# Float64 weights converted through the bits of their high word, with ScalarE and GpSimd taking a share

## The chip, the core and the metric

The kernel runs on one core of a Trainium2 chip. The metric is the device time of one execution in microseconds. TensorE multiplies matrices into PSUM; VectorE (DVE), ScalarE (ACT) and GpSimd (POOL) work on tiles of 128 partitions; SyncE (SP) issues the transfers. PE stands for TensorE's matmuls and PEld for its weight loads.

## The reference

An FFT filter is followed by two MLPs. `x` is (2, 3008, 256); the result of one stage feeds the next.

```python
X = np.fft.rfft(x, axis=1)
y = np.fft.irfft(X * (filt_r + 1j * filt_i)[None], n=3008, axis=1).astype(np.float32)
x = y.reshape(6016, 256)
h = x @ w_in                               # w_in 256 x 2048
x = ((h / (1 + np.exp(-h))) @ w_out).astype(np.float32)
g = x @ w_gate                             # w_gate, w_val 256 x 1536
out = (((g / (1 + np.exp(-g))) * (x @ w_val)) @ w_out2).astype(np.float32)
```

The filter and `x` are float32. The five weight matrices are float64, since `setup_inputs` scales float32 numbers by a float64 factor. No engine here computes in float64, so the kernel has to make float32 of them: it gets each weight as two 32-bit words, the low word first.

## The kernel before

The FFT of length 3008 is done as 64 x 47 by matmuls, batch 0 first (`F0`), in plain float32. Batch 1 (`F1`) is worked off in pieces between the units of the first MLP. Every number that goes into a product of an MLP is split into a high and a low part (two fp32r tiles), and a product is three matmuls: high by high, high by low, low by high.

The first MLP has **units** (`units`): one unit is a block of 512 tokens by 128 hidden columns. `m1_in` makes six matmuls into a PSUM tile of `psp` (four tiles), a Silu on ScalarE gives `u` (L534), ScalarE casts its high part (L514) and VectorE subtracts to get the low part (L515). `m1_out`, six matmuls into `acc`, comes `LAG = 4` units later. The first 32 units go through the weights in four quarters `q`, two token blocks on each; a quarter's weights of `w_in` (`i1`) and `w_out` (`o1`) must be converted by then. All later units use what is there.

The **conversion** goes by half-tiles of 128 x 512 weights, 34 in all: 16 of `i1` and `o1`, 12 of the second MLP's `g` and `v`, 6 of its `o2`. For one half-tile:

- `load_w`: a 512 KB transfer into `raw` (low and high words in turn).
- `conv_a`: VectorE masks the mantissa bits of the high word into `m` (L401), takes the top 16 bits' exponent (L406), clamps it (L407), moves it to float32's place (L408) and joins it with the sign in a tile `scale` (L409), whose other halves were set to zero at the start.
- `conv_m` (L415): ScalarE turns the mantissa into a float, 1 plus m times 2^-20.
- `conv_b`: VectorE adds the low word times 2^-52 (L420), and GpSimd multiplies by `scale` (L421).
- `conv_c`: ScalarE casts the high part `w` (L429), GpSimd subtracts to get the low part (L430).

The order on each engine is the order in which the code issues the operations (`manual_schedule`): by hand until the first unit, then by `todo`, a list of steps by unit index. `weights(i, key, q, step)` puts `load_w` at i - 2, `conv_a` at i, `conv_b` at i + 1 and `conv_c` at i + 2, and the second half `step` units later. The steps of a unit are issued ahead of its matmuls. Engines work in order, so an operation that waits holds up what stands behind it. Tiles named `mid` come from one pool of 35 buffers, in which a new load waits until an old tile has been read.

The other steps that matter here: `s2` filters a spectrum (matmul, then L293 and two L295 on VectorE into `y` and `t2t`, an add L299 on GpSimd); `turn` transposes, and ScalarE copies the result to `tin` (L254); `s4` finishes the inverse transform, ScalarE casting `xh` (L359) and VectorE subtracting (L360). `split_x` splits an input of batch 1 for `s1`, with a cast on ScalarE (L203) and a subtraction of 96 x 1024 on GpSimd (L204).

## Time and profile before

| | us |
|---|---|
| median of three runs | 1226.03 (1224.44 to 1226.59) |
| the profiled execution | 1226.94 |
| span of its trace | 1225.2 |

| engine | busy us | share | instructions |
|---|---|---|---|
| PE | 1198.5 | 98% | 7068 |
| DVE | 752.6 | 61% | 1202 |
| ACT | 651.8 | 53% | 1171 |
| POOL | 443.1 | 36% | 354 |

The span is what the trace covers of one execution; the profiled time has 1.7 us more, of what lies around it. Busy time of PE is that of a pipeline, so that a busy PE need not be at its pace; the granted clock (PEclk, 1.00 is 2.4 GHz) has to be read beside it. A timeline row has the start, the duration, the engine, the line and the operation, and, in brackets, the idle time of the engine ahead of it and the instruction that ended it. The same operation can have different durations at different places. In the table of stretches the engines stand in the order PE, PEld, DVE, ACT, POOL; in the rows of groups the mean is in ns.

### The profile page before, as it was taken

The page shows a single profiled execution, that of the slowest core. Times are in us where ns is not written, and L with a number is a line of the kernel's source. Part 1 is how long each engine was busy: PE and PEld are TensorE (multiplying, and loading weights), DVE is VectorE, ACT ScalarE, POOL GpSimd, SP SyncE. Part 2 cuts the span into 40 slices and gives each one's busy share as a digit, 9 for nine tenths or more (in the row PEclk, how much of TensorE's full clock was granted, in tenths as well). Part 3 has the DMA queues.
Part 4 walks back from the last instruction along what each step waited for, and adds up shares of the span by engine and source line. Part 5 has one row for each costly group of instructions (what it writes and reads, how often), then busy time and mean ns, then how long its engine had stood idle before and what let it go on. Part 6 is the DMA issues. An engine that isn't in the chain of part 4 may idle for free.

```text
span 1225.2 us, 18420 instructions
## 1 busy us (share of the span) xinstructions
PE 1198.5 (98%) x7068; PEld 1049.2 (86%) x7068; DVE 752.6 (61%) x1202; ACT 651.8 (53%) x1171; POOL 443.1 (36%) x354
## 2 busy tenths in 40 slices
PE   8999999999999999999999999999999999999998
PEld 6467678888888888888899999999999999999998
DVE  3989967774245444544425666666666766676664
ACT  2665666565466556556545445445444554444443
POOL 2545643240034233224312443443434434434432
PEclk8999999999999999999999999999999999999999
DMA  9872523331112522412476011010010110110100
GB/s 220 239 208 61 125 78 103 103 95 64 49 55 97 167 69 78 172 43 97 159 282 232 1 36 35 1 36 6 30 36 1 35 35 1 36 35 1 32 18 13
DMA packets 52534, 97.55 MB, mean 80 GB/s; under 512 B 3712, under 2 KB 28800, under 8 KB 52448
## 3 DMA queue, kind: packets, MB, share of 16 engines
q1 hardware_dynamic: 52448, 96.39, 25.4%
q8 instruction: 55, 0.90, 0.3%
q14 instruction: 31, 0.25, 0.1%
HBM read 60.46 MB, written 35.91 MB: 79 GB/s over the span
## 4 chain that ended last, share of the span: by engine, by line
PE 82%; DVE 5%; ACT 3%; issue 2%; POOL 2%; DMA 1%; POOLq 0%; DVEq 0%; ACTq 0%
PE h L507 19%; PE acc L546 19%; PE y L602 11%; PE acc L689 9%; PE xv L602 8%; PE xg L602 7%; PE acc L693 5%; PE s L346 2%; PE s L182 2%; DVE xrl L589 1%; PE s L179 1%; ACT xrh L588 1%; DMA x<-in_xp_dram 1%; ACT xu L588 1%; POOL m L421 1%
## 5 line engine op out<-in xcount | busy, mean ns | idle before, releaser
L546 PE MATMUL acc<-h,w 128*128 128x512 f32 (+1 forms) x1152 | 292.6, 389 | 2.7 <-DVE h L515 2.7
L515 DVE TENSOR_TENSOR h<-u,h 128x512 fp32r<-128x512 f32 (+1 forms) x192 | 156.8, 818 | 217.8 <-ACT h L514 216.4
L507 PE MATMUL h<-xh,w 128*128 128x512 f32 (+1 forms) x768 | 271.0, 394 | 2.6 <-ACT w L429 1.4
L546 PEld LDWEIGHTS acc<-h,w 128*128 128x128 f32 x1152 | 217.0, 189 | 47.2 <-DVE h L515 3.1
L689 PE MATMUL acc<-w,h 128*128 128x512 f32 x564 | 204.8, 397 | 0.0
L602 PE MATMUL y<-xrh,w 128*128 128x256 f32 (+1 forms) x864 | 190.0, 283 | 0.0
L534 ACT ACTIVATE u<-h 128x512 f32<-128x512 f32 (+1 forms) x192 | 112.7, 587 | 123.0 <-PE h L507 121.3
L507 PEld LDWEIGHTS h<-xh,w 128*128 128x128 f32 x768 | 144.7, 189 | 34.3 <-ACT w L429 1.8
L675 POOL TENSOR_TENSOR h<-sg,h 128x512 fp32r<-128x512 f32 (+1 forms) x72 | 91.4, 1270 | 227.9 <-ACT h L672 226.6
L693 PE MATMUL acc<-w,h 128*128 128x256 f32 x564 | 158.3, 281 | 0.1
L602 PEld LDWEIGHTS y<-xrh,w 128*128 128x128 f32 x864 | 148.2, 189 | 4.0
L507 PE MATMUL h<-xl,w 128*128 128x512 f32 (+1 forms) x384 | 149.7, 390 | 0.0
L649 POOL TENSOR_TENSOR c<-u,s 128x512 f32<-128x512 f32 (+1 forms) x72 | 91.6, 1272 | 130.2 <-DVE u L648 128.0
L689 PEld LDWEIGHTS acc<-w,h 128*128 128x128 f32 x564 | 106.1, 188 | 19.2
L602 PE MATMUL y<-xrl,w 128*128 128x256 f32 (+1 forms) x432 | 121.5, 281 | 0.0
L514 ACT CAST h<-u 128x512 fp32r<-128x512 f32 (+1 forms) x192 | 117.5, 612 | 6.2
L693 PEld LDWEIGHTS acc<-w,h 128*128 128x128 f32 x564 | 106.6, 189 | 0.4 <-POOL h L675 0.4
L602 PE MATMUL xv<-xu,w 128*128 128x256 f32 (+1 forms) x648 | 101.5, 283 | 5.5 <-ACT s L627 5.5
L602 PE MATMUL xg<-xu,w 128*128 128x256 f32 (+1 forms) x648 | 100.1, 281 | 0.0
L602 PEld LDWEIGHTS xv<-xu,w 128*128 128x128 f32 x648 | 87.2, 190 | 7.6 <-ACT s L627 7.5
L658 ACT CAST h<-sg 128x512 fp32r<-128x512 f32 (+1 forms) x72 | 44.1, 613 | 92.0 <-DVE sg L650 92.0
L645 ACT ACTIVATE sg<-xg 128x512 f32<-128x512 f32 (+1 forms) x72 | 42.5, 590 | 94.5 <-DVE xg L642 94.5
(109 smaller groups left out, 1918.4 us busy)
## 6 DMA issues: line engine op xcount, KB each, us to landing
raw<-in_w_out_dram SPq DMA_DIRECT2D x14, 512.0 KB, 6.0
zt<-d SPq DMA_DIRECT2D x16, 384.0 KB, 5.1
x<-in_xp_dram SPq DMA_DIRECT2D x15, 384.0 KB, 9.9
d<-z SPq DMA_DIRECT2D x11, 512.0 KB, 3.3
d<-x SPq DMA_DIRECT2D x22, 256.0 KB, 2.2
x<-d SPq DMA_DIRECT2D x11, 512.0 KB, 4.5
out_dram<-ob SPq DMA_DIRECT2D x11, 512.0 KB, 3.2
w<-dw_g SPq DMA_DIRECT2D x9, 512.0 KB, 6.0
```

The source lines that it names most:

```text
L507: nc.tensor.matmul(ps[:, :n], wt[key, f // 4, g][:, wpart, o:o + P], x[xpart][:, g, :n], start=(g == 0 and k == 0), stop=(g == 1 and k == 2),)
L514: nc.scalar.copy(h[:, 0, :n], u[:, :n])
L515: nc.vector.tensor_tensor(h[:, 1, :n], u[:, :n], h[:, 0, :n], op=ALU.subtract)
L534: nc.scalar.activation(u[:, :n], ps[:, :n], AF.Silu)
L546: nc.tensor.matmul(acc[1, t][m][:, :n], w[:, wpart, o:o + 128], h[:, xpart, :n], start=(f == 0 and k == 0), stop=(f == 15 and k == 2),)
L602: nc.tensor.matmul(o, w_op(key, q, j, n, wpart), x, start=(first and k == 0), stop=(last and k == 2), skip_group_check=True,)
L645: nc.scalar.activation(half(g1), half(xs[0]), AF.Silu)
L649: nc.gpsimd.tensor_tensor(c[:, :, 1, :n], u3, s[:, :, 1, :n], op=ALU.add)
L658: nc.scalar.copy(pack(h[:, 0]), half(g1))
L675: nc.gpsimd.tensor_tensor(pack(hs[1][:, 1]), half(g2), pack(hs[1][:, 0]), op=ALU.subtract)
L689: nc.tensor.matmul(a.rearrange("p (l d) -> p l d", l=2), h[:, 0, i * P:(i + 1) * P], w[:, :, f % 2, :], start=(f_at == 0), stop=False, ski ...
L693: nc.tensor.matmul(a[:, D:], h[:, 1, i * P:(i + 1) * P], w[:, 0, f % 2, :], start=False, stop=(f_at == 11), skip_group_check=True,)
```

## The change

The high word of a float64, read as a float32, has a number's sign and the upper exponent and mantissa bits. The new conversion takes its absolute value as a float and clamps it to the range that float32 can hold, cuts off the top exponent bits, shifts the rest left by three, puts sign and top exponent bit back, and adds the low word's upper three bits as an integer.

- `conv_0` is new, on ScalarE: Abs of the high word into `m` (L400 of the new file), and the low word times 2^-29, written as an integer, into `e` (L401).
- `conv_a`, on VectorE: clamp (L406), mask and shift (L407), sign and top bit (L410). Three operations of 512 four-byte words stand for the five before.
- `conv_b` is GpSimd's alone: an add of 32-bit integers (L416) where there was a float multiply. VectorE's L420 of before is gone.
- `conv_c` is as it was, and so are all matmuls and their order.
- `weights` loads at i - 3 and puts `conv_0` at i - 1. SyncE's list has the same 223 rows; in it one load of `raw` moves ahead of one load of `x`, because of the earlier place.
- The `scale` tiles and their three memsets go. `m` has five buffers for four, `e` three.
- In the part by hand, `conv_a` of `i1`'s second half moves behind `s2(6)`, and `conv_0` steps are set ahead of each `conv_a`.

ScalarE's list grows from 1166 to 1200 rows and VectorE's shrinks from 1089 to 961.


VectorE, batch 0's `s2(5)` and what follows, before (`s_410` is `s2(5)`, `s_446` is `s2(6)`):

```order
L293 TENSOR_TENSOR y<-s_410,fr 128x512
L295 TENSOR_TENSOR t2t_112<-s_410,fi 64x512 x2
L401 TENSOR_SCALAR m<-raw 128x512
L406 TENSOR_SCALAR e<-raw 128x512
L407 TENSOR_SCALAR e<-e 128x512
L408 TENSOR_SCALAR e<-e 128x512
L409 SCALAR_TENSOR_TENSOR scale_114<-raw,e 128x512
L293 TENSOR_TENSOR y<-s_446,fr 128x512
L295 TENSOR_TENSOR t2t_111<-s_446,fi 64x512 x2
```

After (`s_402` is `s2(5)`, `s_435` `s2(6)`, `s_464` `s2(7)`):

```order
L292 TENSOR_TENSOR y<-s_402,fr 128x512
L294 TENSOR_TENSOR t2t_112<-s_402,fi 64x512 x2
L292 TENSOR_TENSOR y<-s_435,fr 128x512
L294 TENSOR_TENSOR t2t_111<-s_435,fi 64x512 x2
L406 TENSOR_SCALAR m<-m 128x512
L407 TENSOR_SCALAR m<-m 128x512
L410 SCALAR_TENSOR_TENSOR m<-raw,m 128x512
L292 TENSOR_TENSOR y<-s_464,fr 128x512
L294 TENSOR_TENSOR t2t_112<-s_464,fi 64x512 x2
```

The conversion stands behind `s2(6)` and not ahead of it, and has three operations and not five.

ScalarE at the same place, before: the cast of the first converted half, then the copies of `turn(6)` and `turn(7)`.

```order
L319 COPY z<-s_406 128x512
L266 ACTIVATE fr<-fr 64x512
L429 CAST w<-m 128x512
L254 COPY tin<-turn 128x512 x2
L319 COPY z<-s_442 128x512
```

After:

```order
L318 COPY z<-s_398 128x512
L265 ACTIVATE fr<-fr 64x512
L424 CAST w<-m 128x512
L400 ACTIVATE m<-raw 128x512
L401 ACTIVATE e<-raw 128x512
L253 COPY tin<-turn 128x512 x2
L318 COPY z<-s_431 128x512
```

The two operations of `conv_0` for the second half came in between the cast and the copies to `tin`.

VectorE where the units begin, before: the last subtraction of `s4`, the rest of one conversion, a second one, and the low parts `h` of units 0 and 1.

```order
L360 TENSOR_TENSOR xl<-s_698,xh 128x104
L420 SCALAR_TENSOR_TENSOR m<-raw,m 128x512
L401 TENSOR_SCALAR m<-raw 128x512
L406 TENSOR_SCALAR e<-raw 128x512
L407 TENSOR_SCALAR e<-e 128x512
L408 TENSOR_SCALAR e<-e 128x512
L409 SCALAR_TENSOR_TENSOR scale_114<-raw,e 128x512
L515 TENSOR_TENSOR h<-u,h 128x512 x2
```

After:

```order
L359 TENSOR_TENSOR xl<-s_685,xh 128x104
L406 TENSOR_SCALAR m<-m 128x512
L407 TENSOR_SCALAR m<-m 128x512
L410 SCALAR_TENSOR_TENSOR m<-raw,m 128x512
L510 TENSOR_TENSOR h<-u,h 128x512 x2
```

The rest of the first conversion (L420) is gone, and the second has three operations ahead of unit 0's `h`.

The diff, without its blank lines:

```diff
 F32 = mybir.dt.float32
 F32R = mybir.dt.float32r
 U32 = mybir.dt.uint32
-U16 = mybir.dt.uint16
 AF = mybir.ActivationFunctionType
 ALU = mybir.AluOpType
...
     wt, late = {}, {}
     SRC = {"i1": w_in, "o1": w_out, "g": w_gate, "v": w_val, "o2": w_out2}
-    scale_t = [stp.tile([P, 512, 2], U16, name=f"scale{i}", bufs=1) for i in range(3)]
-    n_half = [0]
+    TINY, HUGE = (float(np.array(h, np.uint32).view(np.float32)) for h in (0x38000000, 0x47EFFFFF))
     raws, parts, pair = {}, {}, {}
     def load_w(key, q, half):
...
                 src[P * half:P * half + P, 1024 * q:1024 * (q + 1)],
             )
-    def conv_a(key, q, half, on_act=True):
+    def conv_0(key, q, half):
         raw = raws[key, q, half]
-        high, top = raw[:, :, 1], raw.bitcast(U16)[:, :, 3]
-        sc = scale_t[n_half[0] % len(scale_t)]
-        n_half[0] += 1
         if key in ("g", "v"):
             if half == 0:
                 pair[key, q] = mid([P, 2, 512], "v2", U32)
             m = pair[key, q][:, half]
         else:
-            m = stp.tile([P, 512], U32, tag="m", name="m", bufs=4)
-        nc.vector.tensor_scalar(m, high, 0xFFFFF, None, op0=ALU.bitwise_and)
-        parts[key, q, half] = m.bitcast(F32), sc
-        if on_act:
-            conv_m(key, q, half)
-        e = stp.tile([P, 512], U16, tag="e", name="e", bufs=1)
-        nc.vector.tensor_scalar(e, top, 0x7FF0, None, op0=ALU.bitwise_and)
-        nc.vector.tensor_scalar(e, e, 896.0 * 16, 1151.0 * 16, op0=ALU.max, op1=ALU.min)
-        nc.vector.tensor_scalar(e, e, 896.0 * 16, 8.0, op0=ALU.subtract, op1=ALU.mult)
+            m = stp.tile([P, 512], U32, tag="m", name="m", bufs=5)
+        e = stp.tile([P, 512], U32, tag="e", name="e", bufs=3)
+        parts[key, q, half] = m.bitcast(F32), e
+        nc.scalar.activation(m.bitcast(F32), raw[:, :, 1].bitcast(F32), AF.Abs)
+        nc.scalar.activation(e, raw[:, :, 0], AF.Copy, scale=2.0 ** -29)
+    def conv_a(key, q, half):
+        v = parts[key, q, half][0]
+        m, high = v.bitcast(U32), raws.pop((key, q, half))[:, :, 1]
+        nc.vector.tensor_scalar(v, v, TINY, HUGE, op0=ALU.max, op1=ALU.min)
+        nc.vector.tensor_scalar(
+            m, m, 0x07FFFFFF, 3, op0=ALU.bitwise_and, op1=ALU.logical_shift_left
+        )
         nc.vector.scalar_tensor_tensor(
-            sc[:, :, 1], top, 0x8000, e, op0=ALU.bitwise_and, op1=ALU.bitwise_or
+            m, high, 0xC0000000, m, op0=ALU.bitwise_and, op1=ALU.bitwise_or
         )
-    def conv_m(key, q, half):
-        v, _ = parts[key, q, half]
-        nc.scalar.activation(v, v.bitcast(U32), AF.Copy, bias=1.0, scale=2.0 ** -20)
     def conv_b(key, q, half):
-        low = raws.pop((key, q, half))[:, :, 0]
-        v, sc = parts[key, q, half]
-        nc.vector.scalar_tensor_tensor(v, low, 2.0 ** -52, v, op0=ALU.mult, op1=ALU.add)
-        nc.gpsimd.tensor_tensor(v, v, sc.rearrange("p f w -> p (f w)").bitcast(F32), op=ALU.mult)
+        v, e = parts[key, q, half]
+        nc.gpsimd.tensor_tensor(v.bitcast(U32), v.bitcast(U32), e, op=ALU.add)
     def conv_c(key, q, half):
         v, _ = parts.pop((key, q, half))
...
     def weights(i, key, q, step=1):
         for half in range(2):
-            at(max(i - 2, 0), load_w, key, q, half)
+            at(max(i - 3, 0), load_w, key, q, half)
+            at(max(i - 1, 0), conv_0, key, q, half)
             for k, fn in enumerate((conv_a, conv_b, conv_c)):
                 at(max(i + k, 0), fn, key, q, half)
             i += step
-    for i, fn, half in ((1, conv_m, 0), (2, conv_b, 0), (3, conv_a, 1), (4, conv_c, 0), (4, conv_b, 1), (6, conv_c, 1)):
+    for i, fn, half in ((1, conv_0, 1), (2, conv_b, 0), (3, conv_a, 1), (4, conv_c, 0), (4, conv_b, 1), (6, conv_c, 1)):
         at(i, fn, "i1", 1, half)
     for q in range(1, 4):
         weights(8 * q - 2, "o1", q, 2)
...
         nc.sync.dma_start(cst[:, 0:96], consts[:, 0:96])
         F0.load_x(0, 4, 4)
         nc.vector.memset(idle, 0.0)
-        first = stp.tile([P, 512], U32, tag="m", name="m", bufs=4).bitcast(F32)
+        first = stp.tile([P, 512], U32, tag="m", name="m", bufs=5).bitcast(F32)
         nc.vector.memset(first[:, :1], 0.0)
         nc.scalar.activation(first[:, :1], first[:, :1], AF.Silu)
         warm(WARM)
-        for sc in scale_t:
-            nc.gpsimd.memset(sc, 0)
         for i in range(1, 4):
             F0.load_x(i)
         nc.sync.dma_start(cst[:, 96:], consts[:, 96:])
...
         s2(0)
         s2(1)
         s1(4, (1,))
+        conv((conv_0, "i1", 0))
         s2(2)
         conv((conv_a, "i1", 0))
         s1(5)
...
         s1(7)
         s3(2)
         s2(5)
-        conv((conv_c, "i1", 0))
+        conv((conv_c, "i1", 0), (conv_0, "i1", 1))
         F0.prep_g(4)
-        conv_a("i1", 0, 1, False)
         turn(6)
         turn(7)
         s3(3)
         s2(6)
+        conv((conv_a, "i1", 1))
         F0.prep_g(5)
         turn(8)
         turn(9)
...
         s2(7)
         turn(10)
         turn(11)
-        conv((conv_m, "i1", 1))
         s3(5)
         s2(8)
         s3(6)
...
         s3(10)
         F1.s1(0, bank_a, (4,))
         F1.store_s1(0)
+        conv((conv_0, "o1", 0))
         for c in range(3):
             s4(c, (0,), bank_a)
         s3(11)
...
         for f in range(4):
             m1_in_first(0, f)
         F1.s1(1, bank_a, (0,))
-        conv((conv_c, "i1", 1))
+        conv((conv_0, "o1", 1), (conv_c, "i1", 1))
         F1.s1(1, bank_a, (4,))
         F1.store_s1(1)
         conv((conv_a, "o1", 1), (conv_b, "o1", 0))
...
         for c in range(3, 6):
             s4(c, (1,), bank_a)
         conv((conv_b, "o1", 1))
-        conv_a("i1", 1, 0, False)
+        conv_0("i1", 1, 0)
+        conv_a("i1", 1, 0)
         at(1, conv_c, "o1", 0, 1)
         for i in range(len(units)):
```


## Rows read from the trace of the kernel before

**Rows 1.** Stretches: length, busy us (count) by engine, granted PE clock, DMA share, GB/s.

```profile
46.27:53.30 7.03, 4.70 (x8) 1.67 (x8) 6.54 (x10) 2.59 (x5) 3.66 (x4) 0.76 0.58 235
...
77.58:84.64 7.06, 4.35 (x14) 3.15 (x12) 6.88 (x11) 3.39 (x7) 2.83 (x2) 0.76 1.03 354
84.64:113.60 28.96, 28.96 (x127) 23.65 (x126) 28.11 (x39) 17.81 (x32) 13.53 (x10) 1.00 0.31 85
113.60:162.74 49.14, 42.83 (x165) 31.09 (x164) 44.46 (x49) 29.06 (x50) 31.92 (x18) 0.93 0.38 97
162.74:300.00 137.26, 137.26 (x625) 112.65 (x624) 89.73 (x100) 85.87 (x145) 41.91 (x25) 1.00 0.26 83
300.00:600.00 300.00, 300.00 (x1377) 247.79 (x1376) 134.37 (x228) 170.69 (x297) 92.01 (x76) 1.00 0.31 100
```

**Rows 2.** Timeline of PE: start, duration, line, operation, idle time before.

```profile
45.41 1.02 PE L179 MATMUL s<-y,cst 128*128 128x512 f32 x2
48.76 1.47 PE L179 MATMUL s<-tin,cst 128*128 128x512 f32 x2 [2.33 <-DVE t2t L295]
...
53.30 1.02 PE L179 MATMUL s<-y,cst 128*128 128x512 f32 x2
54.15 1.02 PE L179 MATMUL s<-tin,cst 128*128 128x512 f32 x2
...
77.58 0.39 PE L546 MATMUL acc<-h,w 128*128 128x512 f32 x1
80.69 2.50 PE L546 MATMUL acc<-h,w 128*128 128x512 f32 x5 [2.71 <-DVE h L515]
82.99 0.63 PE L507 MATMUL h<-xh,w 128*128 128x512 f32 x1
```

**Rows 3.** Timeline of DVE: `conv_a` in gap one, alone, and before unit 0's `h`.

```profile
41.65 0.43 DVE L401 TENSOR_SCALAR m<-raw 128x512 uint32<-128x512 uint32 x1
...
46.61 0.69 DVE L293 TENSOR_TENSOR y<-s,fr 128x512 f32<-128x512 f32 x1
...
65.34 0.42 DVE L401 TENSOR_SCALAR m<-raw 128x512 uint32<-128x512 uint32 x1
...
67.42 0.41 DVE L401 TENSOR_SCALAR m<-raw 128x512 uint32<-128x512 uint32 x1
...
79.96 1.27 DVE L515 TENSOR_TENSOR h<-u,h 128x512 fp32r<-128x512 f32 x2
```

**Rows 4.** Timeline of DVE: one conversion and two units in the full stretch.

```profile
101.85 1.53 DVE L401 TENSOR_SCALAR m<-raw 128x512 uint32<-128x512 uint32 x1
...
104.08 1.27 DVE L408 TENSOR_SCALAR e<-e 128x512 uint16<-128x512 uint16 x1
...
106.69 0.68 DVE L420 SCALAR_TENSOR_TENSOR m<-raw,m 128x512 f32<-128x512 uint32 x1
107.29 0.68 DVE L515 TENSOR_TENSOR h<-u,h 128x512 fp32r<-128x512 f32 x1
107.89 1.51 DVE L401 TENSOR_SCALAR m<-raw 128x512 uint32<-128x512 uint32 x1
```

**Rows 5.** Timeline of POOL: the same multiply undisturbed and in the full stretch.

```profile
62.05 1.27 POOL L421 TENSOR_TENSOR m<-m,scale 128x512 f32<-128x512 f32 x1 [5.01 <-DVE m L420]
...
101.42 1.68 POOL L421 TENSOR_TENSOR m<-m,scale 128x512 f32<-128x512 f32 x1 [2.26 <-DVE m L420]
```

**Rows 6.** Groups of POOL, 113.60 to 162.74: count, busy us, mean ns, idle before.

```profile
L204 POOL TENSOR_TENSOR fl<-x,fh 96x1024 fp32r<-96x1024 f32 x5 | 12.5, 2503 | 1.3 <-ACT fh L203 1.1
```

**Rows 7.** Timeline of ACT around 40 us, and a conversion's scaling copy.

```profile
39.82 0.62 ACT L429 CAST w<-m 128x512 fp32r<-128x512 f32 x1
40.34 1.07 ACT L254 COPY tin<-turn 128x512 f32<-128x512 f32 x2
...
65.80 0.63 ACT L415 ACTIVATE m<-m 128x512 f32<-128x512 uint32 x1 [0.67 <-DVE m L401]
```

**Rows 8.** Instructions on tile `raw`: its loads' time to landing.

```profile
DMA to landing us min/median/max: 3.5/5.5/12.0
```


## The prediction

> **What bounds the kernel now.** I read four views, in this order: the table by stretches, the timeline of TensorE in the stretches that are not full, the timeline of the engine that it waits for there, and the grouped lines of that stretch. In the table the reader should look at TensorE's busy time against the length of the stretch, and at PEclk beside it. From 84.64 to 113.60 and from 162.74 to 600 TensorE is busy all the time at PEclk 1.00 [rows 1]. The first of these has 127 matmuls in 28.96 us, 0.228 us each: that is the full pace of a 512-column product. One unit of the first MLP has 12 of them (six in, six out), 2.74 us, and two units take 5.47 us. Three stretches before 162.74 are not full, and all three show VectorE busy for over nine tenths.
>
> *Gap one, 46.27 to 53.30.* Each pair of spectrum products takes 0.85 us at full pace (53.30 to 54.15). After the pair at 45.41, three pairs should end at 48.8, but the next full-pace pair starts at 53.30 [rows 2]: 4.5 us are lost, partly as idling (2.33 us on VectorE's t2t), partly at PEclk 0.76 [rows 1], that is, some of it at the lower of the two clock levels, 1.2 GHz, after the idling. VectorE was inside the five conversion operations of i1 half 1, 41.65 to 46.61, 4.96 us, while a result waited [rows 3].
>
> *Gap two, 77.58 to 84.64.* The first output product waits 2.71 us for `h` L515, and the six matmuls end at 82.99 and not 1.37 us after 77.58: 4.0 us lost [rows 2]. L515 stands behind another conversion on VectorE and starts at 79.96 [rows 3].
>
> *Gap three, 113.60 to 162.74.* 165 matmuls at 0.228 us are 37.6 us; 49.14 us passed, so some 11 us are lost, again partly at the lower level (PEclk 0.93) [rows 1]. VectorE is busy 44.46 of 49.14.
>
> **Why VectorE is late there.** Two units and one conversion take it from 101.85 to 107.89, 6.04 us against TensorE's 5.47 [rows 4]; it falls behind all through the full stretch, and the bill comes at 113.60. Alone, the five operations of `conv_a` take 2.08 us (65.34 to 67.42) [rows 3]; here L401 takes 1.53 and L408 1.27 [rows 4]. They end just after the GpSimd operation that started at 101.42 and ended at 103.10 [rows 5], which itself took 1.68, not the 1.27 of the row at 62.05: these two engines exclude each other for much of their work. So I add them up. Per half-tile VectorE has 2.08 for `conv_a`, 0.60 for L420 (106.69 to 107.29) and twice 0.60 for L515 (107.29 to 107.89) [rows 4], in all 3.88; GpSimd has twice 1.27 [rows 5], 2.54. The sum 6.42 against 6.04 seen: about 94% of the sum is what the pair needs.
>
> **The change part by part.** *VectorE* loses five narrow operations and L420 and gets three: two tensor-scalar on 512 words, priced by L401's 0.41 alone [rows 3], and one with two tensors, 0.60 as L420 [rows 4]: 1.42 to 1.5 for 2.68, 1.2 us less per half, before any waiting. Its pair sum becomes (1.44 + 1.20 + 2.54) x 0.94 = 4.87 for two units, now below 5.47. With the transforms of batch 1, one every 2.5 units, TensorE has 36 matmuls (8.2 us), and GpSimd one more subtraction of 2.50 us [rows 6]: before (1.25 x 6.42 + 2.50) x 0.94 = 9.9, after (1.25 x 5.18 + 2.50) x 0.94 = 8.4. So five transforms cost 8.5 us too much before and 1 after.
>
> *GpSimd* does an integer add where it did a float multiply. No row has an integer operation there. The nearest is that multiply, 1.27 [rows 5], same shape, two inputs, four-byte words: I take 1.27. The ends are 0.60, what VectorE has for two tensors (L420), and twice the multiply, 2.54; at that end the sum per transform is (1.25 x 6.45 + 2.50) x 0.94 = 9.9, and gap three stays as it is. The three memsets that go ran at the start, when nothing waited for GpSimd: 0.
>
> *ScalarE* gets Abs and a scaling copy for one scaling copy: one operation more per half, priced by L415 (0.63) [rows 7], twice that if reading every other word is slow; below zero is excluded, since an operation is added. In gap three it was busy 29.06 of 49.14 [rows 1]; 6 or 7 halves add 4 us, so it has room. But it works in order, and in three places the pair now stands ahead of something urgent. One is behind the cast at 39.82, ahead of the two `tin` copies at 40.34 [rows 7]: TensorE's next spectrum product comes 1.1 us later (2.5 at the upper price). Another is ahead of the first casts of `s4`, the third ahead of unit 0's Silu; behind that one wait `h`, L510 and the first output product. ACT's list shows one table load, as before, so Abs costs no second one.
>
> *What a rule says of this.* ScalarE takes 0.63 for 512 words, and VectorE 0.41 [rows 3, 7]. The Trainium skill, ScalarE: Activation LUTs, section Rules for kernel authors, says to put such plain arithmetic on VectorE, which it has at up to about three times the rate; the rows show 1.5 times for four-byte words. By that rule the two operations would go to VectorE, the pair sum per transform would be (1.25 x 6.08 + 2.50) x 0.94 = 9.5 against 8.2, and some 5 us of the gain would be gone. The rows speak for ScalarE here, because it is not the engine that is short.
>
> *DMA.* The weight loads are issued one unit earlier and the first reader comes one unit earlier, so two units, 5.5 us, stay between them; landing took 3.5 to 12.0, median 5.5 [rows 8]. ScalarE now waits instead of VectorE. Behind it stand that unit's Silu and cast; TensorE notices only when the four PSUM tiles of `psp` are full, about three units later. On SyncE's list one weight load moves ahead of one `x` load; I put both at 0, and up to 2 us of gap three if the cover fails.
>
> *Where the gains land.* Gap one: VectorE's string from 41.65 loses 4.96 + 0.7 and gets 1.5, up to 2.8 with one wait for GpSimd, and starts 1.0 later because of `tin`; that is 1.9 to 3.1 less, I take 2.6 (ends: -1.3, if the ScalarE delays eat it all, and 4.5). Gap two: L510 stands behind three operations, not five, and VectorE comes there earlier; but ScalarE's pair delays the Silu by 1.2. I take 1.2 left of 4.0: 2.8 (ends 0 and 4.0). Gap three: 1 from the transforms and 1 for ScalarE's order left of 11: 9 (ends 4 and 11). The 18 halves of the second MLP lie in 300 to 600, where TensorE is full and VectorE at 134 of 300 [rows 1]: 0. Past 600 nothing changes.
>
> Sum: 2.6 + 2.8 + 9.0 = 14.4. The profiled execution took 1226.94 us, the median of the runs is 0.9 below it: 1226.94 - 14.4 - 0.9 = 1211.6, so **1212**.
>
> **The rivals.** *ScalarE takes VectorE's place:* the three delays (1.1, 1.2, 1.2) all show in full, and in gap three the cast of `w` waits for GpSimd in front of the next Silu as it does now, so 6 us of 11 stay lost. Gain some 8: 1218. For it: in-order, 60% busy with waits. Against: those waits were for work that VectorE had queued too late. *All gaps close:* 4.5 + 4.0 + 11 = 19.5, 1206.5; against it speaks the `tin` delay. *The gaps belong to the transforms of batch 1* and not to the conversions, and the first two only move: within a microsecond or two, 1225; the period of 6.04 against 5.47 speaks against it. *Slower:* the integer add is dear on GpSimd. It stands in the pair sum in full: at 2.6 us it eats what VectorE saves (1.24 + 1.27); at three times the multiply, 3.8 us, the sum per transform is (1.25 x 7.71 + 2.50) x 0.94 = 11.4, 1.5 over before, 7.6 us for five; and in the stretch from 84.64, 7.25 against 5.47 leaves some 6 more than the lag now. With 5 kept in the first two gaps that gives about 1234. Nothing in the rows shows an integer add, so it can't be excluded.
>
> **How the numbers follow.** Forecast (1208 to 1215) 0.58; all gaps close (below 1208) 0.14; ScalarE's place (1215 to 1221) 0.15; no change 0.06; slower 0.07. About 0.2%, 2.5 us, is what a measurement of this kernel tells from no change: faster 0.87, same 0.06, slower 0.07. An integer add at its upper end would leave the first two gaps' 5.4: 1220.6. The range 1205 to 1221 takes that in, with the forecast and most of its two neighbours, some 0.83.
>
> **What would show it.** Right: PEclk 1.00 and TensorE full from about 75 to 600; the conversion on VectorE in three operations, 1.5 to 2.8 us together; no wait of TensorE for `w`. Wrong: the integer add above 2 us; Abs or the copy above 1 us; TensorE waiting for `u`, `tin` or `xh` of ScalarE, or for a raw weight's load; the gap at 113.60 still there with VectorE idle.

## The result, and the profile after

The changed kernel takes 1211.45 us, median of four runs (1209.42 to 1211.58), beside 1226.31 for the kernel before on the same chip: ratio 0.9878, interval [0.9861, 0.9895]. 1212 was predicted. Run again, the same program gave 1210.40 (ratio 0.9873 [0.9860, 0.9886]). The total is right; none of its three terms is: two were put too small, and the third, up to unit 0, came out with the wrong sign. That is what the experiments are about.

The table by stretches of the changed kernel (columns as in [rows 1]):

```profile
core 0: us, PE busy (x) PEld busy (x) DVE busy (x) ACT busy (x) POOL busy (x), PEclk, DMA share, GB/s
46.00:54.00 8.00, 5.81 (x16) 2.25 (x14) 7.77 (x11) 3.91 (x7) 4.11 (x4) 1.00 0.66 256
75.40:79.05 3.65, 3.20 (x15) 2.24 (x13) 2.06 (x4) 3.59 (x8) 0.53 (x1) 1.00 0.99 253
79.05:111.80 32.75, 32.08 (x140) 25.88 (x139) 30.36 (x32) 27.83 (x49) 21.48 (x14) 1.00 0.43 141
111.80:160.00 48.20, 48.20 (x222) 38.77 (x221) 37.44 (x35) 35.72 (x63) 32.27 (x18) 1.00 0.46 118
```

Set against [rows 1]: PEclk is 1.00 in all of them, and from 111.80 to 160.00, where the kernel before lost some 11 us, TensorE is busy 48.20 of 48.20. In 46 to 54 it still stands for over 2 us, and VectorE is as full as before (7.77 of 8.00).

TensorE's own timeline of the changed kernel (start, duration, line, operation, matmuls; in brackets the idle time ahead and who ended it), its stops of more than 0.2 us up to unit 4, with some rows beside them:

```profile
41.62 1.13 PE L178 MATMUL s<-tin,cst 128*128 128x512 f32 x2 [0.97 <-ACT tin L253]
51.70 1.13 PE L178 MATMUL s<-y,cst 128*128 128x512 f32 x2 [2.04 <-POOL y L298]
69.25 1.55 PE L345 MATMUL s<-cst,zt 96*128 96x94 f32 x12 [0.61 <-DMA zt<-d]
76.20 0.50 PE L502 MATMUL h<-xh,w 128*128 128x512 f32 x1 [0.45 <-ACT u L529]
77.69 1.52 PE L541 MATMUL acc<-h,w 128*128 128x512 f32 x6
80.49 1.53 PE L541 MATMUL acc<-h,w 128*128 128x512 f32 x6
89.29 0.50 PE L502 MATMUL h<-xh,w 128*128 128x512 f32 x1 [0.67 <-POOL w L425]
```

The stop of 2.33 us of [rows 2] has become 0.97 and 2.04; the stop of 2.71 ahead of the first `acc` is gone; a wait for `w` now stands at 89.29, where the kernel before had its waits for `w` at 115.83 (1.38 us) and 117.27 (0.70).

To compare kernels I use four marks on this timeline: the first block of `turn` matmuls after 34 us (T), the first `acc` product of unit 0, of unit 1 and of unit 24. The lengths between them, from the profiled execution of each kernel (before: 39.22, 77.58, 84.64, 169.42; after: 38.75, 77.69, 80.49, 153.92), are called gap one, two and three from here on. Those of the prediction lie inside them: 46.27 to 53.30, 77.58 to 84.64 and 113.60 to 162.74.

| kernel | T at | T to unit 0 (gap one) | unit 0 to 1 (gap two) | unit 1 to 24 (gap three) | unit 24 to end |
|---|---|---|---|---|---|
| before | 39.22 | 38.36 | 7.06 | 84.78 | 1055.8 |
| changed | 38.75 | 38.94 | 2.80 | 73.43 | 1055.6 |
| e12, changed again | 37.67 | 38.93 | 2.78 | 73.24 | 1055.8 |
| e1, no multiply | 40.57 | 38.07 | 4.39 | 74.33 | 1055.5 |
| e2, extra add | 38.86 | 38.90 | 3.50 | 81.38 | 1055.9 |
| e3, on VectorE | 37.48 | 39.85 | 4.35 | 79.26 | 1055.8 |
| e4, old places | 35.72 | 38.23 | 2.74 | 76.27 | 1056.1 |
| e6, i1 later and casts earlier | 41.40 | 34.93 | 2.72 | 74.96 | 1055.6 |
| e7, third operation | 39.29 | 42.39 | 3.45 | 74.15 | 1055.7 |
| e8, late loads | 39.12 | 39.71 | 2.78 | 73.24 | 1055.7 |
| e9, i1 later | 38.67 | 36.69 | 2.77 | 73.32 | 1055.9 |
| e10, i1 and first u later | 38.66 | 42.07 | 3.90 | 73.32 | 1055.9 |
| e11, before, i1 later | 37.79 | 37.73 | 7.66 | 84.54 | 1055.9 |

The change gave 11.35 us in gap three and 4.26 in gap two, lost 0.58 in gap one, and the rest of the 15.7 us between the spans (1225.2 and 1209.5) is T, 0.47, and the end, 0.2. e5 is missing: its profiled execution had a granted clock of 0.75 from end to end, and the same program was run again as e9. Gaps two and three repeat within 0.2 us in the changed kernel, e8 (which edits loads alone), e9 and e12; gap three in e10 too. Gap one does not always repeat: e12 has the changed kernel's length, but e8, whose order up to unit 0 is the same, has 39.71, with PEclk 0.88 in 46 to 54 where the changed kernel had 1.00. T does not repeat either, of which more at the end.

### The profile page after: what moved, and what is told of

It reads as the page before. It is cut to its first block, busy times and chain, and to the rows that moved or that the text cites. A ratio compares the mean times of both kernels' runs of the same rounds, so it can differ in the third digit from the quotient of the medians.

```text
span 1209.5 us, 18403 instructions
## 1 busy us (share of the span) xinstructions
PE 1189.7 (98%) x7068; PEld 1046.4 (87%) x7068; DVE 709.4 (59%) x1100; ACT 668.1 (55%) x1205; POOL 441.5 (37%) x351
## 4 chain that ended last, share of the span: by engine, by line
PE 87%; ACT 4%; DVE 4%; issue 3%; DMA 2%; POOL 1%; SPq 0%; POOLq 0%; DVEq 0%; ACTq 0%
PE acc L541 21%; PE h L502 21%; PE y L597 12%; PE acc L684 9%; PE xv L597 8%; PE xg L597 7%; PE acc L688 5%; PE s L181 2%; PE s L345 2%; DMA fi<-in_fi_dram 1%; DVE xrl L584 1%; DMA raw<-in_w_in_dram 1%; ACT xrh L583 1%; ACT xu L583 1%; DVE sg L645 1%
## 5 line engine op out<-in xcount | busy, mean ns | idle before, releaser
L510 DVE TENSOR_TENSOR h<-u,h 128x512 fp32r<-128x512 f32 (+1 forms) x192 | 168.0, 879 | 244.8 <-ACT h L509 244.4
L541 PE MATMUL acc<-h,w 128*128 128x512 f32 (+1 forms) x1152 | 289.6, 387 | 0.0
```

The lines of the kernel that those rows point to most:

```text
L510: nc.vector.tensor_tensor(h[:, 1, :n], u[:, :n], h[:, 0, :n], op=ALU.subtract)
L541: nc.tensor.matmul(acc[1, t][m][:, :n], w[:, wpart, o:o + 128], h[:, xpart, :n], start=(f == 0 and k == 0), stop=(f == 15 and k == 2),)
```

## Experiments: what gap three is made of

**e1: the kernel before without GpSimd's multiply.** VectorE keeps all its instructions.

```
 def conv_b(key, q, half):
     ...
-    nc.gpsimd.tensor_tensor(v, v, sc.rearrange("p f w -> p (f w)").bitcast(F32), op=ALU.mult)
```

> The kernel before, with GpSimd's multiply by the scale left out of every conversion (the weights stay unscaled, so the output is not the reference's). VectorE's instructions are all as before. Theory A (VectorE and GpSimd exclude each other, so what counts is the sum of both): the sum for two units falls from 6.42 to 3.88 + 1.27 = 5.15, times 0.94 is 4.84, below TensorE's 5.47; with a transform (1.25 x 5.15 + 2.50) x 0.94 = 8.4 against 8.2, as for the changed kernel. The loss at 113.60 to 162.74 goes nearly in full, the first two gaps stay: 1213 to 1217 us. Theory B (VectorE's own five operations are what is too long, GpSimd does not matter): VectorE's 3.88 is unchanged, the loss stays, 1225 to 1227 us.

Measured: 1214.25 us, ratio 0.9889 [0.9874, 0.9903]. Gap three falls from 84.78 to 74.33 although VectorE's five operations are untouched: theory A. That the gaps belong to the transforms of batch 1 is out with it, since none of these was touched. Gap two, which was to stay, falls from 7.06 to 4.39: with the same five operations ahead of it, unit 0's `h` keeps TensorE waiting 1.37 us and not 2.71. VectorE and GpSimd of e1, one conversion:

```profile
89.74 0.42 DVE L406 TENSOR_SCALAR e<-raw 128x512 uint16<-128x512 uint16 x1
93.47 0.42 DVE L401 TENSOR_SCALAR m<-raw 128x512 uint32<-128x512 uint32 x1
98.47 0.42 DVE L401 TENSOR_SCALAR m<-raw 128x512 uint32<-128x512 uint32 x1
98.80 1.52 DVE L406 TENSOR_SCALAR e<-raw 128x512 uint16<-128x512 uint16 x1
```
```profile
98.68 1.36 POOL L429 TENSOR_TENSOR w<-m,w 128x512 fp32r<-128x512 f32 x1 [3.64 <-ACT w L428]
```

One conversion and two units take 5.00 us (93.47 to 98.47), where [rows 4] had 6.04 and the sum promised 4.84. The instruction of 0.42 us (89.74) lasts 1.52 where GpSimd's subtraction starts just ahead of it (98.80, 98.68).

**e2: one more integer add on GpSimd in the changed kernel.**

```
 def conv_b(key, q, half):
     v, e = parts[key, q, half]
     nc.gpsimd.tensor_tensor(v.bitcast(U32), v.bitcast(U32), e, op=ALU.add)
+    nc.gpsimd.tensor_tensor(e, e, e, op=ALU.add)
```

> The changed kernel with one more integer add on GpSimd per half-tile, behind the one it has, on the tile e that nobody reads afterwards (the output stays as it is). Its duration should be that of the add, 1.27 us alone. Theory A (sum of VectorE and GpSimd): 5.18 + 1.27 = 6.45 for two units, times 0.94 is 6.06, as the 6.04 seen before the change; the loss in gap three comes back nearly in full, 11 to 12 us, the first two gaps stay as they now are: 1221 to 1225 us. This is also the run for the rival that a dear integer add makes the change worth little (at 2.5 us it was to eat what VectorE saves). Theory B (VectorE alone): GpSimd's own load is only 2 x 1.27 + 1.27 = 3.8 of 5.47, so nothing moves, 1211 to 1213 us.

Measured: 1219.90 us, ratio 0.9938 [0.9922, 0.9955], a little under the range of theory A. An add whose result nobody reads, on an engine with room (3.8 us of 5.5 by its own count), costs 7.95 us in gap three (81.38 against 73.43): theory B is out. But 11 to 12 were expected. VectorE of e2, then GpSimd:

```profile
94.63 1.26 DVE L406 TENSOR_SCALAR m<-m 128x512 f32<-128x512 f32 x1
97.98 2.39 DVE L511 TENSOR_TENSOR h<-u,h 128x512 fp32r<-128x512 f32 x2
100.29 1.26 DVE L406 TENSOR_SCALAR m<-m 128x512 f32<-128x512 f32 x1
```
```profile
98.14 1.68 POOL L416 TENSOR_TENSOR m<-m,e 128x512 uint32<-128x512 uint32 x1 [1.09 <-DVE m L410]
99.89 1.37 POOL L417 TENSOR_TENSOR e<-e 128x512 uint32<-128x512 uint32 x1
101.22 1.48 POOL L426 TENSOR_TENSOR w<-m,w 128x512 fp32r<-128x512 f32 x1
```

The period is 5.66 us (94.63 to 100.29), not 6.06, only 0.13 over TensorE's two units (2.765 each where it is full). So the factor 0.94 that I carried over is not a constant. The sums and the periods are 5.15 and 5.00 in e1 (one GpSimd operation a half), 6.42 and 6.04 before (two), 6.00 and 5.60 in e3 below (two), 6.45 and 5.66 here (three): the part that overlaps is 0.15, 0.38, 0.40 and 0.79 us, that is 0.15 to 0.26 for each GpSimd operation. In these stretches the two engines shut each other out, but for about 0.2 us for each GpSimd operation.

The Trainium skill, SBUF — State Buffer, section Terms, has this as a port pair that the two share by a lock, held for a whole instruction, where the loser is fully blocked. For the operations of these stretches the trace agrees but for those 0.2 us; some others of VectorE are not held up at all (see gap one).

The period shows the sum; the 7.95 us do not show it alone. In GpSimd's order the added add also stands ahead of other work (99.89, ahead of 101.22). Of the 6.06 us that TensorE waits in gap three of e2 (0.67 in the changed kernel), 4.55 end with GpSimd, the longest wait with `fl`, behind which PEclk is 0.91 in 120 to 140:

```profile
128.46 0.71 PE L181 MATMUL s<-fl,csp 96*96 96x512 f32 x1 [1.91 <-POOL fl L203]
```

How much of the loss comes through GpSimd's own queue and how much through VectorE, e2 does not tell. e3 adds nothing to GpSimd's queue, and loses 5.8 us there all the same.

This run also prices the rival of a dear add: with 2.54 us of integer adds per half the change would still gain 0.62%, near the 1220.6 that the prediction gave for that end.

**e3: Abs and the scaling copy on VectorE.**

```
-    nc.scalar.activation(m.bitcast(F32), raw[:, :, 1].bitcast(F32), AF.Abs)
-    nc.scalar.activation(e, raw[:, :, 0], AF.Copy, scale=2.0 ** -29)
+    nc.vector.tensor_scalar(m, raw[:, :, 1], 0x7FFFFFFF, None, op0=ALU.bitwise_and)
+    nc.vector.tensor_scalar(e, raw[:, :, 0], 29, None, op0=ALU.logical_shift_right)
```

> The changed kernel with Abs and the scaling copy on VectorE, as an and with 0x7FFFFFFF and a shift right by 29, 0.41 us each alone, at the same places in the program. This is what the Trainium skill, ScalarE: Activation LUTs, section Rules for kernel authors, would have: plain arithmetic on VectorE. Theory A (sum of VectorE and GpSimd): 5.18 + 0.82 = 6.0 for two units, times 0.94 is 5.64 against 5.47, and with a transform (1.25 x 6.0 + 2.50) x 0.94 = 9.4 against 8.2: some 5 to 6 us of gap three come back, 1215 to 1219 us. If ScalarE's pair was what cost the most in the changed kernel (its delay of tin, of the first u), the gain there outweighs it: 1209 to 1211 us.

Measured: 1220.80 us, ratio 0.9942 [0.9927, 0.9957]: half of the gain is gone. Gap three has 5.8 us of it, as theory A had, though VectorE's own operations are 3.46 us of 5.53 and GpSimd's 2.54; gap two has another 1.55 and gap one 0.9, which theory A had not, so that the median lies above its range. On VectorE of e3 the operation of 0.41 lasts 1.52, beside a GpSimd operation that started at 96.91 and took 1.68:

```profile
94.13 1.51 DVE L406 TENSOR_SCALAR m<-m 128x512 f32<-128x512 f32 x1
97.35 1.52 DVE L400 TENSOR_SCALAR m<-raw 128x512 uint32<-128x512 uint32 x1
99.73 1.54 DVE L406 TENSOR_SCALAR m<-m 128x512 f32<-128x512 f32 x1
```

The period is 5.60 us (94.13 to 99.73), 5.64 by the sum. The Trainium skill, ScalarE: Activation LUTs, section Rules for kernel authors, would have put the two operations there (its factor of three is for bf16); this run doesn't bear that out for a VectorE that is short.

**e4: the new arithmetic at the old places.** The core of the edit:

```
-            at(max(i - 3, 0), load_w, key, q, half)
-            at(max(i - 1, 0), conv_0, key, q, half)
+            at(max(i - 2, 0), load_w, key, q, half)
+            at(max(i, 0), conv_0, key, q, half)
...
-        conv((conv_c, "i1", 0), (conv_0, "i1", 1))
+        conv((conv_c, "i1", 0))
         F0.prep_g(4)
+        conv((conv_0, "i1", 1), (conv_a, "i1", 1))
         turn(6)
```

> The changed kernel's arithmetic at the places of the kernel before: loads two units ahead and not three, ScalarE's pair right ahead of VectorE's three operations, and those of i1 half 1 ahead of turn(6) as before. Theory A (the arithmetic makes the gain): VectorE now stands up to 1.2 us waiting for ScalarE's pair at each half, but it is the sum with GpSimd that counts and 4.87 + 1.2 = 6.1 is only reached where nothing else of VectorE is queued: 1211 to 1215 us. Rival (the gain hangs on taking ScalarE's pair one unit ahead): VectorE's wait comes on top at every half, two units take 6.1 as before the change, gap three comes back: 1219 to 1224 us.

Measured: 1212.71 us, ratio 0.9881 [0.9865, 0.9896]. The arithmetic makes the gain. The places are worth 2.8 us in gap three (76.27 against 73.43), where VectorE now stands for ScalarE's pair (6.8 us in nine waits); the medians can't tell that apart. The 0.7 us less in gap one is no more than that length moves by itself (e8).

**e8: the loads two units ahead, ScalarE's pair where the change has it.**

```
-            at(max(i - 3, 0), load_w, key, q, half)
+            at(max(i - 2, 0), load_w, key, q, half)
```

> The changed kernel with the weight loads issued two units ahead, as before the change, and not three; ScalarE's pair still comes one unit ahead of VectorE. One unit, 2.77 us, is then between the issue of a load and its first reader; landing took 3.5 to 12.0 us before the change. Theory (ScalarE stands waiting 1 to 9 us at such halves, and TensorE's cover of about three units is used up at the longer ones): 1 to 5 us over the changed kernel, in the stretch from unit 0 to unit 24. Rival (the cover is enough; the earlier load was not needed): within 1 us of the changed kernel.

Measured: 1212.26 us, ratio 0.9869 [0.9852, 0.9886]; gap three 73.24. The earlier loads are worth nothing, so the 2.8 us of e4 are the pair's place.

**e7: a third ScalarE operation.**

```
     nc.scalar.activation(m.bitcast(F32), raw[:, :, 1].bitcast(F32), AF.Abs)
+    nc.scalar.activation(m.bitcast(F32), m.bitcast(F32), AF.Abs)
```

> The changed kernel with a third ScalarE operation in every conversion (Abs of m once more, in place, 0.6 to 0.67 us; the output stays). Theory A (ScalarE has room): the two places where TensorE waits for ScalarE (tin, the first u) grow by 0.65 each, from unit 0 on nothing changes by more than 1 us: 1 to 2.5 us over the changed kernel. Rival (ScalarE, in order and with waits for GpSimd in it, is the next bound): ScalarE's two units hold 2 x 1.25 for Silu and cast, 1.3 for the pair, 0.6 for w and its wait; with 0.65 more the stretch from unit 0 to unit 24 loses 4 us or more: 1217 us or more.

Measured: 1217.26 us, ratio 0.9908 [0.9892, 0.9924]. The time is the rival's, 1217 or more, and not theory A's, but the loss is not where the rival put it: gap three takes 0.72 us and gap two 0.65, so ScalarE has room there, and the rival's 4 us are not to be seen. Ahead of unit 0 it costs 3.45 where 1.3 was expected. TensorE's two waits in e7:

```profile
42.82 1.12 PE L178 MATMUL s<-tin,cst 128*128 128x512 f32 x2 [1.62 <-ACT tin L253]
80.19 0.50 PE L503 MATMUL h<-xh,w 128*128 128x512 f32 x1 [1.47 <-ACT u L530]
```

They grow by 0.65 and 1.02. All waits of gap one together grow by 1.96 us, from 4.40 to 6.36. The other 1.49 are time in which TensorE is busy: PEclk is 0.91 in 40 to 60, 1.00 in the changed kernel. It falls behind the same wait of 2.04 us that the changed kernel has, and the three pairs from 52.89 on take 4.37 us, where three at full pace take 2.58. That this fall comes from the added operation is not shown; e8 had it without one.

## Experiments: why gap one gave nothing

VectorE in gap one of the changed kernel, then GpSimd:

```profile
42.79 0.69 DVE L292 TENSOR_TENSOR y<-s,fr 128x512 f32<-128x512 f32 x1 [1.63 <-PE s L178]
44.84 0.41 DVE L406 TENSOR_SCALAR m<-m 128x512 f32<-128x512 f32 x1
45.29 1.39 DVE L407 TENSOR_SCALAR m<-m 128x512 uint32<-128x512 uint32 x1
46.71 1.41 DVE L410 SCALAR_TENSOR_TENSOR m<-raw,m 128x512 uint32<-128x512 uint32 x1
48.14 0.69 DVE L292 TENSOR_TENSOR y<-s,fr 128x512 f32<-128x512 f32 x1
```
```profile
45.07 1.32 POOL L298 TENSOR_TENSOR y<-y,t2t 128x512 f32<-128x512 f32 x1 [0.26 <-DVE t2t L294]
46.35 1.22 POOL L270 TENSOR_TENSOR fi<-fi,cst 128x512 f32<-128x512 f32 x1
```

The three operations take 3.30 us (44.84 to 48.14), 1.5 alone: two GpSimd operations stand in their way, not the one I allowed for. Ahead of them VectorE idles 1.63, 0.97 of it TensorE's wait for `tin`. What it saved over [rows 3], 4.96 - 3.30, is spent by that idle time.

Not all of VectorE's work is shut out, though. In the same gap, VectorE's two lines of `s2` and a GpSimd add:

```profile
50.27 0.69 DVE L292 TENSOR_TENSOR y<-s,fr 128x512 f32<-128x512 f32 x1
50.97 1.39 DVE L294 TENSOR_TENSOR t2t<-s,fi 64x512 f32<-64x512 f32 x2
```
```profile
50.38 1.26 POOL L298 TENSOR_TENSOR y<-y,t2t 128x512 f32<-128x512 f32 x1 [2.80 <-DVE t2t L294]
```

The add runs beside both, and none of the three is slower than alone: the 24 instructions of L292 in the whole program last 0.690 to 0.693 us, the 48 of L294 0.683 to 0.694, beside GpSimd or not. Both lines read `s`, which lies in PSUM; the conversion and the low parts `h`, which stretch, read SBUF alone. That this is the reason was not tried. The sum of the two engines holds for the operations that stretch, and only for them.

**e5 and e9: the conversion of i1 half 1 out of the gap**:

```
-        conv((conv_c, "i1", 0), (conv_0, "i1", 1))
+        conv((conv_c, "i1", 0))
...
-        conv((conv_a, "i1", 1))
         F0.prep_g(5)
...
         turn(11)
+        conv((conv_0, "i1", 1))
...
-        conv((conv_b, "i1", 1))
+        conv((conv_a, "i1", 1), (conv_b, "i1", 1))
```

> The changed kernel with the conversion of i1 half 1 taken out of gap one: ScalarE's pair behind the tin copies of turn(11), VectorE's three operations behind the last y of s2(11). From the third transposition of turn (38.75 us in the changed kernel's profile) to the first output product of unit 0 (77.69) it took 38.94 us, before the change 38.36: gap one gave nothing. Theory C (the conversion sits where VectorE is the bound: it is busy without a break from 43.51 to 59.9, and the tin copies wait 1.0 us behind ScalarE's pair): that stretch becomes 1.0 + 2.0 us shorter, 35.5 to 37 us, and the median falls by 2 to 3 us below the changed kernel's. Rival (what comes next is late anyway: the second half of zt, which TensorE waits for at 69.25, or the first u): 38.5 to 39.5 us, median within 1 us of the changed kernel's. From unit 0 on nothing should move (76.2 us from unit 0 to unit 24).

> The kernel of the earlier run with i1 half 1 later, whose profiled execution had a granted clock of 0.75 from end to end. Seen so far where i1 half 1 is later together with a second move: 34.93 us from the third transposition of turn to unit 0's first output product (38.94 in the changed kernel) and 77.68 from unit 0 to unit 24 (76.23). Theory C: the move of i1 half 1 alone gives 3 to 3.6 of the 4.0 (35.3 to 36 us, the rest being the wait for the first u, 0.45), and leaves the stretch from unit 0 at 76.0 to 76.6: the median falls 2.5 to 4 us below the changed kernel run beside it. Rival (the second move made it): 38 us or more.

e5: ratio 0.9853 [0.9826, 0.9881]. e9, the same program: 1208.99 us (1204.85 to 1213.70), ratio 0.9857 [0.9836, 0.9878]. Gap one falls to 36.69, 2.2 us less, and the three operations behind the last `y` take 1.6 us in all (56.74 to 58.38). That is between theory C, 35.3 to 36, and its rival, 38 or more. Beside the changed kernel on that chip (e12, 1210.40) the median is 1.4 us lower, less than the 2.5 to 4 expected, and the intervals overlap: that the move gains anything is not shown by the times. TensorE of e9, and what is late next:

```profile
57.16 1.58 PE L345 MATMUL s<-cst,zt 96*128 96x94 f32 x12 [0.92 <-DMA zt<-d]
73.86 0.50 PE L502 MATMUL h<-xh,w 128*128 128x512 f32 x1 [0.80 <-ACT u L529]
```

Both waits are new or longer (0.45 for `u` in the changed kernel): the first half of `zt` comes by DMA when it comes.

**e6: the same, the next weight's pair behind the first Silu, and the casts of `w` one unit earlier.**

```
-    for i, fn, half in ((1, conv_0, 1), (2, conv_b, 0), (3, conv_a, 1), (4, conv_c, 0), (4, conv_b, 1), (6, conv_c, 1)):
+    for i, fn, half in ((1, conv_0, 0), (1, conv_a, 0), (2, conv_b, 0), (2, conv_0, 1), (3, conv_a, 1), (3, conv_c, 0), (4, conv_b, 1), (5, conv_c, 1)):
...
-        conv_0("i1", 1, 0)
-        conv_a("i1", 1, 0)
```

> As the run with i1 half 1 later, and in addition the conversion of the next weight (i1, q = 1): ScalarE's pair of half 0 and VectorE's three go behind unit 0's Silu and cast (which waited for them, 0.45 us of TensorE), ScalarE's pair of half 1 one unit later, and both casts of w one unit earlier (TensorE waited 0.67 us at 88.6 for the second). If these waits are what they seem, 0.5 us less up to unit 0 and 0.7 to 0.9 less between unit 0 and unit 24 (75.4 in place of 76.2): together 3 to 4 us below the changed kernel's median. If the casts now stand waiting for GpSimd in front of Silu, it is no better than the run with i1 half 1 later alone, within 0.5 us.

Measured: 1211.50 us, ratio 0.9856 [0.9834, 0.9878]. Gap one is 34.93, the shortest seen (4.0 less), but unit 1 to 24 takes 1.5 more, and T came at 41.40. By the ratios no better than e9, and no 3 to 4 us below the changed kernel.

**e10: e9 with the next weight's half 0 behind the first Silu, the casts left alone.**

```
-    for i, fn, half in ((1, conv_0, 1), (2, conv_b, 0), ...
+    for i, fn, half in ((1, conv_0, 0), (1, conv_a, 0), (1, conv_0, 1), (2, conv_b, 0), ...
...
-        conv_0("i1", 1, 0)
-        conv_a("i1", 1, 0)
```

> As the run with i1 half 1 later, and the conversion of i1, q = 1, half 0 behind unit 0's Silu and cast; the rest of the order as in the changed kernel. Theory: 0.45 us less up to unit 0 (34.9 us), and from unit 0 on 76 to 76.8, since the casts of w stay where they are: 0 to 0.5 us below the run with i1 half 1 later. Rival (the 1.45 us that the stretch from unit 0 lost in the run with both moves comes from this one): 77.5 us there, and 1 us above it.

Measured: 1211.18 us (1204.96 to 1215.83), ratio 0.9872 [0.9846, 0.9899]. Unit 1 to 24 is 73.32, so e6's loss there came from the casts, or from half 1's pair, which e6 moved too. From unit 0 to unit 24, which the expectation speaks of, it is 77.22, above the theory's 76.8 and just under the rival's 77.5: gap two is 3.90, with a wait of 0.88 us for `u` at 83.13. Gap one of the profiled execution, the slowest of the six, is 42.07. TensorE of e10, and its line by stretches:

```profile
58.76 2.88 PE L345 MATMUL s<-cst,zt 96*128 96x94 f32 x12 [2.53 <-DMA zt<-d]
61.42 1.97 PE L178 MATMUL s<-y,cst 128*128 128x512 f32 x2
63.19 2.71 PE L345 MATMUL s<-cst,zt 96*128 96x94 f32 x12
```
```profile
58.00:70.00 12.00, 11.24 (x38) 9.33 (x39) 4.23 (x12) 2.80 (x9) 1.26 (x1) 0.57 0.71 200
```

TensorE waited 2.53 us for `zt`, and then ran at PEclk 0.57, that is mostly at 1.2 GHz, to about 69: the 12 matmuls of 63.19 take 2.71, those of e9 at their place 1.47. Waits with a lower clock behind them were part of gaps one and two of the kernel before, too [rows 1, 2]. Up to some 3 us before unit 0, e10 has e9's order on every engine, and T came at the same time (38.66 and 38.67); but the loads of `zt` were issued at 54.76, in e9 at 53.14. So most of the 5.4 us between the two profiles is chance, and not the edit. A kernel that comes early to a transfer can pay for it twice, and that fits the wide spread of e9's and e10's times.

**e11: the kernel before, with its i1 half 1 moved the same way.**

```
-        conv_a("i1", 0, 1, False)
         turn(6)
...
-        conv((conv_m, "i1", 1))
...
-        conv((conv_b, "i1", 1))
+        conv_a("i1", 0, 1, False)
+        conv((conv_m, "i1", 1), (conv_b, "i1", 1))
```

> The kernel before, its arithmetic unchanged, with the conversion of i1 half 1 moved as in that run: VectorE's five operations and ScalarE's one behind the last y of s2(11), not ahead of turn(6). If gap one is a matter of the place and not of the arithmetic, the stretch from the third transposition to unit 0 falls from 38.36 to 34.5 to 36.5 us here too, and gaps two and three stay (91.8 us from unit 0 to unit 24): median 2 to 4 us below the kernel before. Rival (the old conversion, 2.1 us on VectorE and one wait for ScalarE, now delays xl and with it the first h as much): within 1 us of the kernel before.

Measured: 1225.69 us, ratio 0.9999 [0.9988, 1.0010]: no gain. Gap one is 0.63 shorter, gap two 0.60 longer; `zt` was 1.53 us late, and PEclk fell to 0.93 in 60 to 80. So the rival's time is right, though not its reason: TensorE has no wait for `xl` in gap one. In this execution the place was no lever by itself, since `zt` and `h` set the pace next.

**e12: the changed kernel beside e9 to e11.**

> The changed kernel itself, on the same chip as the three runs beside it, since its first product of unit 0 lay at 38.94 us behind the third transposition while that transposition itself lay anywhere from 35.7 to 41.4 us in the kernels so far, whose programs are alike up to there. Expected: 38.5 to 39.7 us for the first stretch, 76.0 to 76.4 from unit 0 to unit 24, 1055.5 to 1056.2 from there to the end; the ratio to the kernel before again 0.986 to 0.9895. If the stretches moved by more than this from one execution to the next, differences of less than 1 us between kernels could not be read from single profiles.

Measured: 1210.40 us, ratio 0.9873; all stretches as expected. T, for which nothing was expected, lay at 37.67.

## Why the prediction was right, and where it was not

- **What bounds it: right** for the conversion and the units. VectorE and GpSimd as one resource is what e1, e2 and e3 show, each from another side. One of the readings behind it was loose: L401 ends just after the GpSimd operation named there, but L408 (104.08 to 105.35) after another, which started at 103.83 and took 1.37. The period of two units was to be 4.87. In the changed kernel's full stretch it is 4.80, with VectorE now waiting for ScalarE's `h` in it, while GpSimd's add runs:

```profile
97.74 0.41 DVE L406 TENSOR_SCALAR m<-m 128x512 f32<-128x512 f32 x1
99.62 0.69 DVE L410 SCALAR_TENSOR_TENSOR m<-raw,m 128x512 uint32<-128x512 uint32 x1
101.39 1.22 DVE L510 TENSOR_TENSOR h<-u,h 128x512 fp32r<-128x512 f32 x1 [0.48 <-ACT h L509]
102.54 0.41 DVE L406 TENSOR_SCALAR m<-m 128x512 f32<-128x512 f32 x1
```

- **Gap three: too small.** 9.0 predicted, 11.35 measured in unit 1 to 24, with 0.9 us of a new wait for `w` taken off. The 1 us left for ScalarE's order and the 1 for the transforms did not show, and the gap itself was some 12 and not 11.
- **Gap two: too small.** 2.8 predicted, 4.26 measured, all that there was. TensorE waits 0.45 for the first `u` (76.20), not 1.2, and by the marks this wait falls in gap one. The fewer operations ahead of `h` are not the whole cause: e1 keeps all five and gains 2.67 without the multiply.
- **Gap one: wrong, 2.6 predicted, -0.6 measured.** The step that failed is "1.9 to 3.1 less, I take 2.6". Its `tin` delay of 1.1 was right (0.97); the conversion's 1.5, "up to 2.8 with one wait for GpSimd", was 3.30 with two waits; and the 0.7 that it takes off beside the 4.96 was not there to take: by its size it is L420, and in the kernel before this half's L420 ran later:

```profile
61.29 0.68 DVE L420 SCALAR_TENSOR_TENSOR m<-raw,m 128x512 f32<-128x512 uint32 x1
```

With what was measured, the same sum is 4.96 - 3.30 - 0.97 = 0.69, and 0.57 us less is what shows at the first `h` (63.05 against 64.09, that is 24.30 and 24.87 behind T). It went to longer waits for `zt` (0.61, before 0.19) and the first `u` (0.45, before none). Over the whole of gap one TensorE waits 4.40 us, before 2.72, and needs 1.10 us less for its work, with PEclk 1.00 and not 0.96: -0.58 in all. The lower end, -1.3, "if the ScalarE delays eat it all", names the case. The sum that I used for gap three was not used for the conversion here, although GpSimd is busy for half of that stretch (4.11 of 8.00).

- **The prices: right.** The integer add takes 1.26 us alone and 1.67 where it starts beside VectorE, as the multiply ([rows 5]: 1.27 and 1.68). Abs and copy take 0.67 and 0.66, 0.63 predicted. The add alone, then the changed kernel's groups between 84 and 160 us (line, engine, operation, count, busy us, mean ns):

```profile
55.89 1.26 POOL L416 TENSOR_TENSOR m<-m,e 128x512 uint32<-128x512 uint32 x1
```

```profile
L416 POOL TENSOR_TENSOR m<-m,e 128x512 uint32<-128x512 uint32 x11 | 18.5, 1680 | 11.5 <-DVE m L410 11.5
L400 ACT ACTIVATE m<-raw 128x512 f32<-128x512 f32 x10 | 6.7, 666 | 0.0
L401 ACT ACTIVATE e<-raw 128x512 uint32<-128x512 uint32 x10 | 6.6, 659 | 0.0
```

- **Loads at 0, the second MLP at 0: right** (e8; unit 24 to the end is 1055.5 to 1056.1 in all kernels). **No wait for `w`: wrong**, 0.67 us.
- **The sum:** 2.6 + 2.8 + 9.0 = 14.4 against -0.6 + 4.3 + 11.35 = 15.0, and 0.7 from T and the end. The errors, 3.2 too much and 3.8 too little, nearly cancel, and that is luck; the time came out within 1 us because of it.

## What to carry to other kernels

See in the trace which of VectorE's operations get longer beside GpSimd's (here those that read SBUF alone, not those that read PSUM). Add these and GpSimd's work per period, and allow some 0.2 us of overlap for each GpSimd operation; an operation moved to ScalarE leaves this sum, one that is moved to VectorE enters it (e3). Use the sum wherever such operations meet, in a ramp as in a steady stretch. A stretch that gets shorter is worth what the next late thing leaves of it: in the ramp that was a DMA and a Silu, in the steady stretch one wait for `w`.

## What was not expected of the hardware

The mark T lay between 35.72 and 41.40 us in thirteen profiled executions whose programs differ little up to there. The stretches of e4 and e6, by the same columns as above, e4 first:

```profile
24.00:32.00 8.00, 6.78 (x39) 4.92 (x39) 7.20 (x11) 5.20 (x10) 4.89 (x4) 1.00 1.05 266
32.00:40.00 8.00, 7.03 (x38) 4.45 (x37) 6.82 (x10) 6.61 (x13) 6.46 (x6) 1.00 1.05 304
```
```profile
24.00:32.00 8.00, 5.65 (x27) 3.48 (x27) 6.13 (x9) 3.49 (x7) 4.85 (x4) 0.91 1.05 260
32.00:40.00 8.00, 8.00 (x36) 6.14 (x36) 4.92 (x8) 3.63 (x8) 2.52 (x3) 0.66 1.06 257
```

The DMA engines are full in both; in e6 TensorE waits longer ahead of its products at 17.30 and 29.18 (2.24 and 2.35 us; in e4 1.87 and 1.22 ahead of 16.08 and 26.89) and then gets PEclk 0.66. So 5.7 us between two profiles can come from the start alone. Gaps two and three can be compared to better than that, the spans can't, and gap one only with care: it moved by 0.8 us between the changed kernel and e8 and by 5.4 between e9 and e10, with the same order of work nearly to its end. What makes TensorE fall to 1.2 GHz in one execution and not in another stays open.
